# Exponentials with their sums on ScalarE, the sign of converted weights as an integer, and another order in the first block

## The chip, the core and the metric

The kernel runs on one core of a Trainium2 chip. The core has five engines that take their instructions in order, each from its own queue: PE (TensorE, matmuls and transposes), DVE (VectorE), ACT (ScalarE), POOL (GpSimd) and SP, which here only issues DMAs. PE writes to PSUM; DVE and ACT read and write PSUM and SBUF; POOL has SBUF alone. Engines wait for each other by semaphores. The metric is the device time of one execution in microseconds; lower is better.

## What is computed

Attention without a score matrix, and then two feed-forward layers, in float32, for 8 batches of 576 tokens, 8 heads of 64 columns:

```python
q_s = exp(q - max(q, axis=-1)); q_s = q_s / (sum(q_s, axis=-1) + 1e-9)     # over the 64 columns
k_s = exp(k - max(k, axis=2));  k_s = k_s / (sum(k_s, axis=2) + 1e-9)      # over the 576 tokens
kv  = einsum('bhsd,bhse->bhde', k_s, v)
x   = einsum('bhsd,bhde->bhse', q_s, kv)            # then (4608, 512): heads side by side
x   = (silu(x @ w_gate) * (x @ w_val)) @ w_out      # d_ff 1536
out = elu(x @ w_in) @ w_out2                        # d_ff 2048
```

The weights come as float64. Inputs q, k and v are float32.

## The kernel before

The tokens are cut into 9 blocks of 512. Every product is made of three matmuls: each factor is held as a high part, rounded to TensorE's float32 form, and the remainder, and high x high, high x remainder and remainder x high are summed in PSUM (`mm3` and `proj`, L632 to L636 for the projections, L613 to L615 for the second product). The feed-forward layers come in three passes over the 9 blocks: "a" is the first half of d_ff of the first layer, "b" its second half, "2" the second layer. Pass "a" is where attention lies: while block i goes through its six steps ff of three parts s (gate projection, val projection, the second product of the step before), the attention of block i + 1 is put between them by the tables `PLAN0` (for i = 0), `PLAN1` and `PLAN`, which name the part (ff, s) at which a step is issued. So the instructions of an engine stand in the order in which this program writes them; nothing moves later.

The weights are converted on the chip, 68 chunks of 128x512, by `conv()`, which in block 0 is called at each part and takes one chunk a stage further. The stages: `conv_scale` (ACT) multiplies the upper 32-bit word of each float64, read as a float32, by 2^-112, which shifts its exponent; `conv_bits` (DVE, L154, L157, L161) shifts the result left by three bits, puts the sign bit back and fills in the top bits of the lower word; `conv_split` makes the high part on ACT (L182) and the remainder on POOL (L183).

The attention steps of a block: `kmax` is the maximum of keys over tokens of a partition (DVE), `k1` transposes it on PE and reduces it (DVE), `k2` spreads it by PE over the partitions again (mb); `ks` subtracts it from the keys (ke), `kexp` is the exponential (ACT), and `kv` 40 small matmuls for two halves of the heads, whose result is divided by the sum into bd. For the queries: `qmax` (DVE), `qsub` (POOL in the first two blocks), `qexp` (ACT), `qsum` (DVE), `qnorm` (POOL there), then transposes `qT` and the product `xT`, whose result is split into x and its remainder.

Block 0's attention is `first_block()`, written out by hand ahead of the stream: nothing but small work can be on PE until x is there. The key's and value's halves (heads 0 to 3 and 4 to 7) are loaded one after the other on SP's queue. The first gate projection (`lo_last`) takes x's high parts first.

Of the kernel before, what the change touches and what calls it, by code (L numbers as in the profile page):

```python
# [7 lines left out]
FP32 = mybir.dt.float32  # L8
F32R = mybir.dt.float32r
U32 = mybir.dt.uint32  # L10
I64 = mybir.dt.int64
ACTF = mybir.ActivationFunctionType
ALU = mybir.AluOpType
AX = mybir.AxisListType
# [3 lines left out]
def kernel(  # L18
# [23 lines left out]
    nc = tc.nc  # L42
    B, H, S, D = q.shape
# [7 lines left out]
    NREST = S - 512  # L51
    NW1, NW2, NRAW, NCG, NCD = 20, 12, 3, 3, 4
# [79 lines left out]

    def conv_scale(wait=0):
        n = stage["scale"]
        if n >= stage["load"] or n >= stage["bits"] + NCG or calls[0] < loaded[n] + wait:
            return
        stage["scale"] += 1
        g = cv_p.tile([128, 512], U32, tag="cg", name="cg", bufs=NCG)
        nc.scalar.activation(
            out=g.bitcast(FP32), in_=raws[n][:, :, 1].bitcast(FP32), func=ACTF.Copy,  # L140
            scale=2.0 ** -112,
        )
        gs[n] = g

    def conv_bits():
        n = stage["bits"]
        if n >= stage["scale"] or n >= free[0] + NCD:
            return  # L150
        stage["bits"] += 1
        g = gs.pop(n)
        s = ps_c.tile([128, 512], U32, tag="c", name="c")
        nc.vector.tensor_scalar(  # L154
            s, g, 3, 0x7FFFFFFF, op0=ALU.logical_shift_left, op1=ALU.bitwise_and
        )
        nc.vector.scalar_tensor_tensor(  # L157
            out=s, in0=g, scalar=0x80000000, in1=s, op0=ALU.bitwise_and, op1=ALU.bitwise_or
        )
        d = cv_p.tile([128, 512], U32, tag="cd", name="cd", bufs=NCD)  # L160
        nc.vector.scalar_tensor_tensor(  # L161
            out=d, in0=raws.pop(n)[:, :, 0], scalar=29, in1=s,
            op0=ALU.logical_shift_right, op1=ALU.bitwise_or,
        )
        ds[n] = d

    def conv_split(eng):
        n = stage["split"]
# [98 lines left out]
    def kmax(b):  # L267
        t, r = k_t[b]
        m = at1.tile([128, H, D], FP32, tag="km", name="km")
        nc.vector.tensor_tensor(m, t[:, :, 0, :], t[:, :, 1, :], op=ALU.max)  # L270
        nc.vector.tensor_tensor(m, m, t[:, :, 2, :], op=ALU.max)
        nc.vector.tensor_tensor(m, m, t[:, :, 3, :], op=ALU.max)
        nc.vector.tensor_tensor(m[0:NREST], m[0:NREST], r, op=ALU.max)
        km_t[b] = m

# [69 lines left out]
            op=ALU.mult,  # L345
        )

    qr_t, qn_t = {}, {}
# [12 lines left out]

    def qexp(t, n):
        x = q_t[t][:, 4 * n:4 * n + 4]
        nc.scalar.activation(out=x, in_=x, func=ACTF.Exp)

    def qsum(t, n):
        h = slice(4 * n, 4 * n + 4)
        nc.vector.tensor_reduce(out=qr_t[t][:, h], in_=q_t[t][:, h], axis=AX.X, op=ALU.add)

    def qnorm(t, n, eng=None):  # L370
        h = slice(4 * n, 4 * n + 4)
        x = q_t[t][:, h]
        r = qr_t[t][:, h]
# [97 lines left out]
    def first_block():  # L471
# [22 lines left out]
        def km(n, eng):  # L494
            h = hs[n]
            eng.tensor_tensor(m[:, h], kt[:, h, 0, :], kt[:, h, 1, :], op=ALU.max)
            eng.tensor_tensor(m[:, h], m[:, h], kt[:, h, 2, :], op=ALU.max)
            eng.tensor_tensor(m[:, h], m[:, h], kt[:, h, 3, :], op=ALU.max)
            eng.tensor_tensor(m[0:NREST, h], m[0:NREST, h], kr[:, h], op=ALU.max)

        def turn(n, src):
            ps = bank()[:, 0:256]
# [28 lines left out]
        def vcopy(n):  # L531
            h = slice(4 * n, 4 * n + 4)
            src = st.rearrange("p h j d -> p j h d")
            nc.scalar.activation(out=vtile[:, 0:4, h, 0:D], in_=src[:, :, h], func=ACTF.Copy)

        load(kt, k, 0)
        nc.sync.dma_start(out=kr, in_=k[0, :, 512:S, :].rearrange("h p d -> p h d"))
        load(kt, k, 1)
        load(st, v, 0)
        load_half(0)  # L540
        load_half(1)
# [10 lines left out]
        nc.gpsimd.memset(ke[NREST:128, 4], 0.0)  # L552
        nc.gpsimd.memset(vtile[NREST:128, 4], 0.0)
        nc.gpsimd.memset(vtile[:, :, :, D:D + 1], 1.0)
        km(0, nc.vector)
        p0 = turn1(0)
        km(1, nc.vector)
        p1 = turn1(1)
        p0 = kmc(0, p0)
        p1 = kmc(1, p1)  # L560
        vcopy(0)
        ksub(0, p0)
        qmax(0, 0)
        qsub(0, 0, nc.gpsimd)
        kexp(0)
        kv(0, 0, 0)
        qmax(0, 1)
        qsub(0, 1, nc.gpsimd)
        vcopy(1)
        qexp(0, 0)  # L570
        ksub(1, p1)
        kexp(1)
        kv(0, 1, 0)
        qsum(0, 0)
        qexp(0, 1)
        qnorm(0, 0, nc.gpsimd)
        conv_scale()
        conv_scale()
        kv(0, 0, 1)
        qT(0, 0)  # L580
        qT(0, 2)
        qsum(0, 1)
        qnorm(0, 1, nc.gpsimd)
        kv(0, 1, 1)
        conv_bits()
        conv_split(nc.gpsimd)
        qT(0, 1)
        qT(0, 3)
        xT(0, 0, 0)
        conv_scale()  # L590
        xT(0, 0, 1)
        xT(0, 1, 1)
        load_q(1)
        xT(0, 2, 0)
        conv_bits()
        conv_split(nc.gpsimd)
        xT(0, 2, 1)
        xT(0, 3, 1)
        conv_scale()
# [174 lines left out]
    def load_next(ph, i):  # L774
# [14 lines left out]
        "kmax": (4, 2), "qmax": (5, 2),  # L789
    }  # L790
    PLAN0 = {
# [16 lines left out]
    def steps(i):  # L808
        t, u = i + 1, i + 2
        e = nc.gpsimd if i == 0 else nc.vector  # L810
        st = {}
        if i == 1:
            st["store0"] = lambda: store_x(0)
        if t < B:
            st["kmax0"] = lambda: kmax(t)
            st["k1"] = lambda: k1(t)
            st["k2"] = lambda: (k2(t), t + 1 < B and t > 1 and load_k(t + 1))
            st["ks0"] = lambda: ks(t, (0, 1), nc.gpsimd)
            st["ks1"] = lambda: (ks(t, (2, 3), nc.gpsimd), ks(t, (4,), nc.vector))
            st["load_v"] = lambda: load_v(t)  # L820
            st["load_k2"] = lambda: load_k(t + 1)
            st["load_q2"] = lambda: load_q(t + 1)
            st["load_v2"] = lambda: load_v(t + 1)
            st["kexp"] = lambda: kexp(t)
            st["kv0"] = lambda: kv(t, 0)
            st["kv1"] = lambda: (
                kv(t, 1),
                t + 1 < B and t > 1 and load_v(t + 1),
            )
        if t < NB:  # L830
            st["qmax0"] = lambda: (qmax(t, 0), qmax(t, 1))
            st["sub0"] = lambda: qsub(t, 0, e)
            st["sub1"] = lambda: qsub(t, 1, e)
            st["exp0"] = lambda: qexp(t, 0)
            st["exp1"] = lambda: qexp(t, 1)
            st["sum"] = lambda: (qsum(t, 0), qsum(t, 1))
            st["norm0"] = lambda: qnorm(t, 0, e)
            st["norm1"] = lambda: (qnorm(t, 1, e), t + 1 < NB and t > 1 and load_q(t + 1))
            for n in range(KD):
                st[f"qT{n}"] = lambda n=n: qT(t, n)  # L840
                st[f"xT{n}"] = lambda n=n: xT(t, n)
            st["store"] = lambda: store_x(t)
        if u < B:
# [137 lines left out]
```

## Time and profile before

| | us |
|---|---|
| median of 3 runs (1791.27 to 1791.88) | 1791.45 |
| profiled execution, its own time | 1792.23 |
| its span, first to last instruction | 1790.5 |
| PE busy | 1752.0 |
| DVE busy | 924.9 |
| ACT busy | 856.0 |
| POOL busy | 173.1 |

PE is the engine that is busy nearly all the time. The span begins with some 30 us in which it has only small matmuls; the first matmul of the stream starts at 29.63. An engine's busy share says nothing on what it delays; for that the waits of PE, and the chain that leads to each, have to be read.

### The profile page before, as it was taken

The page shows a single profiled execution, that of the slowest core. Times are in us where ns is not written, and L with a number is a line of the kernel's source. Part 1 is how long each engine was busy: PE and PEld are TensorE (multiplying, and loading weights), DVE is VectorE, ACT ScalarE, POOL GpSimd, SP SyncE. Part 2 cuts the span into 40 slices and gives each one's busy share as a digit, 9 for nine tenths or more (in the row PEclk, how much of TensorE's full clock was granted, in tenths as well). Part 3 has the DMA queues.
Part 4 walks back from the last instruction along what each step waited for, and adds up shares of the span by engine and source line. Part 5 has one row for each costly group of instructions (what it writes and reads, how often), then busy time and mean ns, then how long its engine had stood idle before and what let it go on. Part 6 is the DMA issues. An engine that isn't in the chain of part 4 may idle for free.

```text
span 1790.5 us, 21046 instructions
## 1 busy us (share of the span) xinstructions
PE 1752.0 (98%) x8448; PEld 1433.3 (80%) x8448; DVE 924.9 (52%) x1383; ACT 856.0 (48%) x1466; POOL 173.1 (10%) x135
## 2 busy tenths in 40 slices
PE   6799999999999999999999999999999999999999
PEld 4577888888888888888888788888888888888887
DVE  6866567556577666534346744333433343334343
ACT  4563544534465454433334654444444444444444
POOL 3630000000022222111113300000000000000000
PEclk9899999999999999999999999999999999999999
DMA  9274534341255344433334401010101010101000
GB/s 273 80 228 102 147 100 124 105 114 65 78 192 176 129 171 168 165 118 118 118 118 164 174 3 71 1 71 1 71 1 71 1 71 1 71 1 71 1 24 24
DMA packets 103106, 169.13 MB, mean 94 GB/s; under 512 B 41696, under 2 KB 80608, under 8 KB 98528
## 3 DMA queue, kind: packets, MB, share of 16 engines
q1 hardware_dynamic: 103008, 167.79, 28.5%
q8 instruction: 66, 1.08, 0.3%
q14 instruction: 32, 0.26, 0.0%
HBM read 111.15 MB, written 56.62 MB: 94 GB/s over the span
## 4 chain that ended last, share of the span: by engine, by line
PE 90%; issue 2%; DVE 2%; POOL 2%; ACT 2%; DMA 1%; SPq 1%; POOLq 0%; DVEq 0%; ACTq 0%
PE a L632 17%; PE a L633 17%; PE a L636 17%; PE y L613 12%; PE y L615 12%; PE y L614 12%; POOL w L183 1%; PE t L451 1%; DMA ev<-in_v 1%; PE t L390 1%; SPq L242 0%; PE t L331 0%; PE c L331 0%; DMA xs<-x 0%; POOL ke L310 0%
## 5 line engine op out<-in xcount | busy, mean ns | idle before, releaser
L632 PE MATMUL a<-x,w 128*128 128x512 f32 x1432 | 562.8, 393 | 1.5 <-DVE th L688 1.2
L633 PE MATMUL a<-x,w 128*128 128x512 f32 x1432 | 558.9, 390 | 0.7 <-POOL x L463 0.7
L636 PE MATMUL a<-x,w 128*128 128x512 f32 x1432 | 382.8, 389 | 0.0
L645 ACT ACTIVATE g<-th 128x512 fp32r<-128x512 f32 x252 | 159.3, 632 | 442.4 <-DVE th L673 226.3
L632 PEld LDWEIGHTS a<-x,w 128*128 128x128 f32 x1432 | 269.8, 188 | 60.7 <-DVE th L688 2.0
L633 PEld LDWEIGHTS a<-x,w 128*128 128x128 f32 x1432 | 269.8, 188 | 56.2 <-POOL x L463 1.2
L636 PEld LDWEIGHTS a<-x,w 128*128 128x128 f32 x1432 | 268.8, 188 | 55.8
L685 DVE SCALAR_TENSOR_TENSOR th<-e,th 128x512 f32<-128x512 f32 x144 | 100.9, 701 | 356.6 <-ACT e L684 356.6
L651 DVE TENSOR_TENSOR g<-th,g 128x512 fp32r<-128x512 f32 x246 | 176.2, 716 | 136.7 <-ACT g L645 136.6
L613 PE MATMUL y<-w,g 128*128 128x512 f32 x576 | 224.1, 389 | 0.0
L615 PE MATMUL y<-w,g 128*128 128x512 f32 x576 | 224.1, 389 | 0.0
L614 PE MATMUL y<-w,g 128*128 128x512 f32 x576 | 224.1, 389 | 0.0
L667 DVE SCALAR_TENSOR_TENSOR th<-th,e 128x512 f32<-128x512 f32 x108 | 77.3, 715 | 274.6 <-ACT th L663 274.6
L682 ACT ACTIVATE e<-a 128x512 f32<-128x512 f32 x144 | 86.1, 598 | 183.4 <-PE a L636 183.4
L613 PE MATMUL y<-g,w 128*128 128x512 f32 x432 | 171.8, 398 | 0.0
L660 ACT ACTIVATE e<-a 128x512 f32<-128x512 f32 x107 | 64.1, 599 | 224.4 <-PE a L636 224.3
L614 PE MATMUL y<-g,w 128*128 128x512 f32 x432 | 169.0, 391 | 0.0
L615 PE MATMUL y<-g,w 128*128 128x512 f32 x432 | 169.0, 391 | 0.0
L183 POOL TENSOR_TENSOR w<-cd,w 128x512 fp32r<-128x512 f32 x68 | 91.6, 1349 | 624.8 <-ACT w L182 604.1
L613 PEld LDWEIGHTS y<-w,g 128*128 128x128 f32 x576 | 108.2, 188 | 22.6
L615 PEld LDWEIGHTS y<-w,g 128*128 128x128 f32 x576 | 108.1, 188 | 22.5
L614 PEld LDWEIGHTS y<-w,g 128*128 128x128 f32 x576 | 108.1, 188 | 22.3
(137 smaller groups left out, 1705.7 us busy)
## 6 DMA issues: line engine op xcount, KB each, us to landing
xs<-x SPq DMA_DIRECT2D x9, 2048.0 KB, 6.3
x<-xs SPq DMA_DIRECT2D x36, 512.0 KB, 6.2
ys<-yst SPq DMA_DIRECT2D x36, 512.0 KB, 3.7
x<-ys SPq DMA_DIRECT2D x36, 512.0 KB, 7.2
raw<-in_moe_w_out SPq DMA_DIRECT2D x26, 512.0 KB, 3.3
yp<-ev SPq DMA_DIRECT2D x9, 1024.0 KB, 4.0
ev<-yp SPq DMA_DIRECT2D x9, 1024.0 KB, 7.9
raw<-in_moe_w_in SPq DMA_DIRECT2D x16, 512.0 KB, 4.0
```

The source lines that it names most:

```text
L183: eng.tensor_tensor(w[:, 1, :], df, w[:, 0, :].bitcast(FP32), op=ALU.subtract)
L613: nc.tensor.matmul(out=ps, lhsT=wh, rhs=xh, start=first, stop=False)
L614: nc.tensor.matmul(out=ps, lhsT=wh, rhs=xl, start=False, stop=False)
L615: nc.tensor.matmul(out=ps, lhsT=wl, rhs=xh, start=False, stop=last)
L632: nc.tensor.matmul(out=ps, lhsT=wh, rhs=x[:, c, 0, :], start=(c == 0), stop=False)
L633: nc.tensor.matmul(out=ps, lhsT=wh, rhs=x[:, c, 1, :], start=False, stop=False)
L636: nc.tensor.matmul(out=ps, lhsT=wl, rhs=x[:, c, 0, :], start=False, stop=(c == KD - 1))
L645: nc.scalar.activation(out=gt[:, 0, :], in_=src, func=ACTF.Copy)
L651: (eng or nc.vector).tensor_tensor(gt[:, 1, :], src, gt[:, 0, :].bitcast(FP32), op=ALU.subtract)
L667: nc.vector.scalar_tensor_tensor(out=t, in0=t, scalar=1.0, in1=e, op0=ALU.add, op1=ALU.mult)
L682: nc.scalar.activation(out=e, in_=h, func=ACTF.Relu, scale=-1.0)
L685: nc.vector.scalar_tensor_tensor(out=t, in0=e, scalar=1.0, in1=t, op0=ALU.add, op1=ALU.mult)
```

## The change

Four things change. In the conversion, ACT makes, beside the scaled word, a second tile by a Prelu with a large slope, written as an int32: positive and negative values saturate there, so that with the shifted word it gives the sign; DVE then needs two operations for a chunk where it had three. In blocks 0 and 1 the queries' subtraction, exponential and sum become 32 ACT operations a block: `qexp_sum` takes one head and one of four token groups, 64 columns, with the negated maximum as a bias and the sum as a second output (`accum_out`). The keys' maximum of batch 1 is one reduction. And `first_block` and `PLAN0` are in another order; the copies of v move from ACT to POOL, and products of `qnorm` in the first block from POOL to DVE.

```diff
     def conv_scale(wait=0):
...
+        d = cv_p.tile([128, 512], U32, tag="cd", name="cd", bufs=NCD)
+        nc.scalar.activation(
+            out=d.bitcast(I32), in_=g.bitcast(FP32), func=ACTF.Prelu, scale=2.0 ** 90,
+            alpha=2.0 ** 100,
+        )
...
     def conv_bits():
...
-        nc.vector.tensor_scalar(
-            s, g, 3, 0x7FFFFFFF, op0=ALU.logical_shift_left, op1=ALU.bitwise_and
-        )
         nc.vector.scalar_tensor_tensor(
-            out=s, in0=g, scalar=0x80000000, in1=s, op0=ALU.bitwise_and, op1=ALU.bitwise_or
-        )
+            out=s, in0=g, scalar=3, in1=d, op0=ALU.logical_shift_left, op1=ALU.bitwise_or
+        )
...
     def kmax(b):
...
+        if b == 1:
+            nc.vector.tensor_reduce(
+                out=m, in_=t.rearrange("p h j d -> p h d j"), axis=AX.X, op=ALU.max
+            )
...
+    def qmaxn(t, n):
+        qmax(t, n)
+        h = slice(4 * n, 4 * n + 4)
+        nc.vector.tensor_scalar(qr_t[t][:, h], qr_t[t][:, h], -1.0, None, op0=ALU.mult)
+
+    def qexp_sum(t, hs):
+        x, r = q_t[t], qr_t[t]
+        if t not in qs_t:
+            qs_t[t] = at1.tile([128, H, 4], FP32, tag="qs", name="qs")
+        for h in hs:
+            for j in range(4):
+                nc.scalar.activation(
+                    out=x[:, h, j], in_=x[:, h, j], func=ACTF.Exp, bias=r[:, h, j:j + 1],
+                    accum_out=qs_t[t][:, h, j:j + 1],
+                )
...
     def vcopy(n):
...
-            nc.scalar.activation(out=vtile[:, 0:4, h, 0:D], in_=src[:, :, h], func=ACTF.Copy)
+            nc.gpsimd.tensor_copy(vtile[:, 0:4, h, 0:D], src[:, :, h])
 
         load(kt, k, 0)
+        load(kt, k, 1)
         nc.sync.dma_start(out=kr, in_=k[0, :, 512:S, :].rearrange("h p d -> p h d"))
-        load(kt, k, 1)
...
-        km(0, nc.vector)
+        km(0)
+        km(1)
+        nc.vector.tensor_tensor(m[0:NREST], m[0:NREST], kr, op=ALU.max)
...
     PLAN0 = {
...
-        "exp0": (1, 2), "ks1": (2, 0), "sub1": (2, 0), "exp1": (2, 1), "kexp": (2, 1),
+        "k2": (2, 0), "ks0": (2, 0), "ea2": (2, 0), "ks1": (2, 1), "ea3": (2, 1),
...
-            st["ks1"] = lambda: (ks(t, (2, 3), nc.gpsimd), ks(t, (4,), nc.vector))
+            st["ks1"] = lambda: ks(t, (2, 3, 4), nc.gpsimd)
...
+            st["qmaxn"] = lambda: (qmaxn(t, 0), qmaxn(t, 1))
+            for n in range(4):
+                st[f"ea{n}"] = lambda n=n: qexp_sum(t, (2 * n, 2 * n + 1))
```

On ACT, in the first block, before (ke are the keys' exponentials, q the queries', cg the scaled word, vtile the values, qT the transposed queries, x the first projection's input):

```order
L534 ACTIVATE vtile<-ev 128x4x4x64
L529 ACTIVATE ke<-ke 128x256 x4
L529 ACTIVATE ke<-ke 64x256
L534 ACTIVATE vtile<-ev 128x4x4x64
L364 ACTIVATE q<-q 128x1024
L529 ACTIVATE ke<-ke 128x256 x4
L529 ACTIVATE ke<-ke 64x256
L364 ACTIVATE q<-q 128x1024
L139 ACTIVATE cg<-raw 128x512 x2
```

On ACT, at the same place in the first block, now (qs are the sums, cd the Prelu's output):

```order
L555 ACTIVATE ke<-ke 128x256 x4
L555 ACTIVATE ke<-ke 64x256
L388 ACTIVATE q,qs<-q,qr 128x64 x16
L140 ACTIVATE cg<-raw 128x512
L147 ACTIVATE cd<-cg 128x512
L555 ACTIVATE ke<-ke 128x256 x4
L555 ACTIVATE ke<-ke 64x256
L388 ACTIVATE q,qs<-q,qr 128x64 x16
L425 ACTIVATE qT_313<-t 128x512
```

The copies of v are gone from ACT, each exponential of the queries is 16 instructions, and the first chunk's two conversion operations stand ahead of the second half of the keys.

On the same engine, ahead of the second batch's keys in block 0's stream (w is a weight's high part, e and th belong to the gates, g is the split gate product, mb the spread maximum), before:

```order
L299 ACTIVATE mb<-t 128x512
L364 ACTIVATE q<-q 128x1024
L182 ACTIVATE w<-cd 128x512
L139 ACTIVATE cg<-raw 128x512
L660 ACTIVATE e<-a 128x512
L661 ACTIVATE th<-a 128x512
L662 ACTIVATE e<-e 128x512
L663 ACTIVATE th<-th 128x512
L182 ACTIVATE w<-cd 128x512
L139 ACTIVATE cg<-raw 128x512
L364 ACTIVATE q<-q 128x1024
L315 ACTIVATE ke<-ke 128x2048
```

On ACT, at the same place of the stream, now:

```order
L309 ACTIVATE mb<-t 128x512
L388 ACTIVATE q,qs<-q,qr 128x64 x8
L187 ACTIVATE w<-cd 128x512
L140 ACTIVATE cg<-raw 128x512
L147 ACTIVATE cd<-cg 128x512
L388 ACTIVATE q,qs<-q,qr 128x64 x8
L668 ACTIVATE g<-th 128x512
L187 ACTIVATE w<-cd 128x512
L140 ACTIVATE cg<-raw 128x512
L147 ACTIVATE cd<-cg 128x512
L325 ACTIVATE ke<-ke 128x2048
L326 ACTIVATE ke<-ke 64x512
```

Two other groups of eight stand ahead of mb; kexp (L325) comes behind all 32, and behind the split of the third g, which had stood after it.

## Rows read from the trace of the kernel before

**Rows 1.** The page: busy time, share of the span and instructions of each engine.
```profile
PE 1752.0 (98%) x8448; PEld 1433.3 (80%) x8448; DVE 924.9 (52%) x1383; ACT 856.0 (48%) x1466; POOL 173.1 (10%) x135
```
**Rows 2.** Waits of PE: what waited for what: us in total, times, longest.
```profile
PE t L280 <- DVE km L273: 7.6, 1, 7.6
PE t L331 <- ACT ke L315: 3.1, 1, 3.1
...
PE a L632 <- DVE th L688: 1.2, 2, 0.6
...
PE t L390 <- DVE bd L343: 0.9, 1, 0.9
```
**Rows 3.** Stretches: us, busy us of each engine (instructions), granted clock, DMA.
```profile
0.00:34.52 34.52, 18.61 (x133) 12.45 (x133) 20.94 (x46) 16.69 (x30) 11.55 (x15) 1.00 1.02 284
34.52:75.29 40.77, 27.41 (x106) 21.48 (x104) 37.60 (x51) 20.73 (x35) 23.59 (x17) 0.83 0.48 121
75.29:86.77 11.48, 10.58 (x108) 8.52 (x109) 8.98 (x18) 6.25 (x12) 9.20 (x6) 0.85 0.27 91
```
**Rows 4.** Timeline of PE: start, us, line, out<-in, count, idle before.
```profile
25.36 1.97 PE L390 MATMUL y<-ident,qn 128*128 128x128 f32 x8 [0.52 <-POOL qn L378]
...
31.12 3.56 PE L625 MATMUL y<-x,w 128*128 128x512 f32 x10 [0.54 <-ACT x L433]
34.52 0.40 PE L632 MATMUL y<-x,w 128*128 128x512 f32 x1
...
75.29 1.88 PE L331 MATMUL t<-vtile,ke 128*64 128x65 f32 x40 [3.15 <-ACT ke L315]
```
**Rows 5.** Timeline of DVE, block 0 and the next.
```profile
43.28 0.69 DVE L154 TENSOR_SCALAR c<-cg 128x512 uint32<-128x512 uint32 x1
44.00 0.69 DVE L157 SCALAR_TENSOR_TENSOR c<-cg,c 128x512 uint32<-128x512 uint32 x1
...
46.48 1.64 DVE L271 TENSOR_TENSOR km<-km,k 128x512 f32<-128x512 f32 x1
...
107.70 0.69 DVE L271 TENSOR_TENSOR km<-km,k 128x512 f32<-128x512 f32 x1
```
**Rows 6.** Timeline of DVE, first block.
```profile
13.70 2.33 DVE L354 TENSOR_REDUCE qr<-q 128x16 f32<-128x1024 f32 x2
```
**Rows 7.** Timeline of ACT, first block and the first gate.
```profile
18.94 1.63 ACT L529 ACTIVATE ke<-ke 128x256 f32<-128x256 f32 x5
20.47 1.04 ACT L364 ACTIVATE q<-q 128x1024 f32<-128x1024 f32 x1
...
28.95 1.08 ACT L433 ACTIVATE x<-y 128x512 fp32r<-128x512 f32 x2 [0.99 <-PE y L451]
...
38.26 0.63 ACT L662 ACTIVATE e<-e 128x512 f32<-128x512 f32 x1
38.78 0.63 ACT L663 ACTIVATE th<-th 128x512 f32<-128x512 f32 x1
```
**Rows 8.** Groups by shape, ACT, up to 75.3: busy us, mean ns.
```profile
L946 ACT ACTIVATE warm<-warm 128x1 f32<-128x1 f32 x1 | 0.2, 203 | 0.0
...
L315 ACT ACTIVATE ke<-ke 128x2048 f32<-128x2048 f32 x1 | 1.9, 1894 | 0.0
```
**Rows 9.** Timeline of ACT in pass "2": a Tanh that needs the Relu.
```profile
1201.36 0.60 ACT L682 ACTIVATE e<-a 128x512 f32<-128x512 f32 x1 [1.40 <-PE a L636]
1201.99 0.63 ACT L683 ACTIVATE th<-e 128x512 f32<-128x512 f32 x1
```
**Rows 10.** Timeline of POOL, block 0.
```profile
45.85 1.72 POOL L651 TENSOR_TENSOR g<-th,g 128x512 fp32r<-128x512 f32 x1
...
70.44 1.90 POOL L360 TENSOR_TENSOR q<-q,qr 128x1024 f32<-128x1024 f32 x1
```
**Rows 11.** The tile raw up to 40 us: duration and start of issues; time to landing.
```profile
L125 SPq DMA_DIRECT2D raw<-in_moe_w_gate x3: 1100/1256/1276, 9.1 to 36.3; - x3
...
DMA to landing us min/median/max: 8.5/10.1/11.7
```

More of the change, by code (lines that the diff above doesn't have):

```diff
@@ L11 @@
 I64 = mybir.dt.int64
+I32 = mybir.dt.int32
 ACTF = mybir.ActivationFunctionType
@@ L134, in conv_scale @@
         n = stage["scale"]
-        if n >= stage["load"] or n >= stage["bits"] + NCG or calls[0] < loaded[n] + wait:
+        if n >= stage["load"] or n >= stage["bits"] + NCG or n >= stage["split"] + NCD or calls[0] < loaded[n] + wait:
             return
@@ L142, in conv_scale @@
         )
+        d = cv_p.tile([128, 512], U32, tag="cd", name="cd", bufs=NCD)
[3 more added lines that the diff above has]
+        )
         gs[n] = g
+        ds[n] = d
     def conv_bits():
         n = stage["bits"]
-        if n >= stage["scale"] or n >= free[0] + NCD:
+        if n >= stage["scale"]:
             return
@@ L153, in conv_bits @@
         s = ps_c.tile([128, 512], U32, tag="c", name="c")
-        nc.vector.tensor_scalar(
-            s, g, 3, 0x7FFFFFFF, op0=ALU.logical_shift_left, op1=ALU.bitwise_and
-        )
-        nc.vector.scalar_tensor_tensor(
-            out=s, in0=g, scalar=0x80000000, in1=s, op0=ALU.bitwise_and, op1=ALU.bitwise_or
-        )
-        d = cv_p.tile([128, 512], U32, tag="cd", name="cd", bufs=NCD)
+        d = ds[n]
+        nc.vector.scalar_tensor_tensor(
+            out=s, in0=g, scalar=3, in1=d, op0=ALU.logical_shift_left, op1=ALU.bitwise_or
+        )
         nc.vector.scalar_tensor_tensor(
@@ L164, in conv_bits @@
         )
-        ds[n] = d
     def conv_split(eng):
@@ L269, in kmax @@
         m = at1.tile([128, H, D], FP32, tag="km", name="km")
-        nc.vector.tensor_tensor(m, t[:, :, 0, :], t[:, :, 1, :], op=ALU.max)
-        nc.vector.tensor_tensor(m, m, t[:, :, 2, :], op=ALU.max)
-        nc.vector.tensor_tensor(m, m, t[:, :, 3, :], op=ALU.max)
+        if b == 1:
+            nc.vector.tensor_reduce(
+                out=m, in_=t.rearrange("p h j d -> p h d j"), axis=AX.X, op=ALU.max
+            )
+        else:
+            nc.vector.tensor_tensor(m, t[:, :, 0, :], t[:, :, 1, :], op=ALU.max)
+            nc.vector.tensor_tensor(m, m, t[:, :, 2, :], op=ALU.max)
+            nc.vector.tensor_tensor(m, m, t[:, :, 3, :], op=ALU.max)
         nc.vector.tensor_tensor(m[0:NREST], m[0:NREST], r, op=ALU.max)
@@ L346, in kv @@
         )
-    qr_t, qn_t = {}, {}
+    qr_t, qn_t, qs_t = {}, {}, {}
     def qmax(t, n):
@@ L372, in qnorm @@
         x = q_t[t][:, h]
-        r = qr_t[t][:, h]
+        r = (qs_t if t in qs_t else qr_t)[t][:, h]
         nc.vector.tensor_scalar(r, r, 1e-9, None, op0=ALU.add)
@@ L492, in load, with km @@
             )
-        def km(n, eng):
+        def km(n):
             h = hs[n]
[L496 to L499, printed above, removed]
+            nc.vector.tensor_tensor(m[:, h], kt[:, h, 0, :], kt[:, h, 1, :], op=ALU.max)
+            nc.vector.tensor_tensor(m[:, h], m[:, h], kt[:, h, 2, :], op=ALU.max)
+            nc.vector.tensor_tensor(m[:, h], m[:, h], kt[:, h, 3, :], op=ALU.max)
         def turn(n, src):
@@ L554, in first_block @@
         nc.gpsimd.memset(vtile[:, :, :, D:D + 1], 1.0)
-        km(0, nc.vector)
+        km(0)
+        km(1)
+        nc.vector.tensor_tensor(m[0:NREST], m[0:NREST], kr, op=ALU.max)
         p0 = turn1(0)
-        km(1, nc.vector)
         p1 = turn1(1)
@@ L562, in first_block @@
         ksub(0, p0)
-        qmax(0, 0)
-        qsub(0, 0, nc.gpsimd)
+        qmaxn(0, 0)
         kexp(0)
         kv(0, 0, 0)
-        qmax(0, 1)
-        qsub(0, 1, nc.gpsimd)
+        ksub(1, p1)
+        qmaxn(0, 1)
+        qexp_sum(0, range(0, 4))
         vcopy(1)
-        qexp(0, 0)
-        ksub(1, p1)
+        conv_scale()
         kexp(1)
         kv(0, 1, 0)
[L574 to L578, printed above, removed]
+        qnorm(0, 0)
         kv(0, 0, 1)
+        qexp_sum(0, range(4, 8))
         qT(0, 0)
         qT(0, 2)
-        qsum(0, 1)
-        qnorm(0, 1, nc.gpsimd)
+        conv_bits()
         kv(0, 1, 1)
+        qnorm(0, 1)
+        conv_scale()
         conv_bits()
-        conv_split(nc.gpsimd)
         qT(0, 1)
         qT(0, 3)
+        conv_split(nc.gpsimd)
         xT(0, 0, 0)
-        conv_scale()
         xT(0, 0, 1)
         xT(0, 1, 1)
+        conv_split(nc.gpsimd)
+        conv_scale()
         load_q(1)
         xT(0, 2, 0)
-        conv_bits()
-        conv_split(nc.gpsimd)
         xT(0, 2, 1)
```

4 rows, old and new, of the table PLAN0 are left out of this document.

## The prediction, as it was put on record

> **What bounds the kernel now.** I read the page first: TensorE is busy for 98% of the span [rows 1], so only a stretch in which it waits can give or take time. The list of its waits came next. They are few: the two largest inside the stream are 7.6 us for the maxima of the second batch's keys (km, L273) and 3.1 us for their exponentials (ke, L315), both in the first block of tokens; of what comes after 121 us, only two waits for th (L688) of 0.6 us each stand there [rows 2]. The table by stage says the same: of 121 us TensorE works 18.6 of the first 34.5 and 27.4 of the next 40.8 [rows 3]; behind that it is full. So the change is decided in the first 90 us, in two pieces: the start, up to the val projection at 34.52, and from there to kv0, the 40 small matmuls at 75.29 that wait for ke [rows 4].
>
> **What costs nothing.** Each of the 68 weight chunks loses one of three VectorE operations (0.72 from start to start) [rows 5] and gains a Prelu of 512 columns on ScalarE. Over the program this moves some 49 us off VectorE and 35 us on to ScalarE. After 121 us neither shows: TensorE has hardly a wait there [rows 2], and ScalarE is busy 48% [rows 1]. The new maximum of the keys reads 2048 elements in one reduction, twice the 1.2 us that 1024 take, where the second of three operations alone took 1.64 [rows 5, 6]. It also stands two steps earlier than the transposes that need it, so the wait of 7.6 us goes. What is late next is the question.
>
> **The price on which all hangs.** In the first two blocks POOL subtracts, ScalarE exponentiates (two of 1.04 us a block [rows 7]) and VectorE sums. All this becomes 32 exponentials a block on ScalarE, each of 64 columns, with the maximum as a bias read from memory and a sum written out. The trace has no such instruction. From the rows: 1.04 us for 1024 columns and 1.89 for 2048 give 0.83 ns a column, so 64 columns take 0.24 us; the Exp and the Abs of a gate start 0.52 apart at 0.63 each, so 0.11 overlap and the least step is 0.134 us [rows 7, 8]. The sum must be read out after the last element, by a small operation (128x1 took 203 ns [rows 8], so about 0.10 in step). Where one ScalarE operation needs the other's result, the overlap is lost: Tanh starts 0.63 after a Relu of 0.60 [rows 9]. So: 0.24, a gap of 0.03 and 0.10 make 0.37 us each. The ends are 0.134 (bias and read-out free) and 0.46 (nothing overlaps: 0.241 + 0.203 + gaps). I take 0.37, since Relu to Tanh is the nearest row. In 16 that is 5.9 us, where one exponential of 1.04 stood.
>
> The Trainium skill, ScalarE: Activation LUTs, section "What ACT_TABLE_LOAD costs", says that a per-partition pointer operand adds about 93 ns to an ACTIVATE. No row here has such an operand. By that rule my 0.37 would be 0.46 and the time by the sum below 1801 us; with the read-out overlapped it would be 0.33, and 1794.
>
> **The start.** The exponentials of the first half can start when the first maximum, which started at 13.70 (1.2), and a negation of 16 columns (an estimate: 0.2, as 128x1 on ScalarE) are through, at 15.1 [rows 6, 8]. The reordered key loads leave that start where it is: both halves' maxima are one chain now, but the second half lands about as much sooner as the remainder lands later. The two copies of v go to POOL, which has nothing else to do there; the later one is not needed before the second kv. From 15.1 ScalarE holds in a row: 16 exponentials (5.9), scale and Prelu of a chunk (0.65 + 0.52 = 1.17: the Prelu needs the scale's result, so as Relu to Tanh), the keys' exponentials (1.63 [rows 7]), and 16 more (5.9): it ends at 29.7. Before, the second exponential ended at 21.5 [rows 7]. Then two small operations and the product on VectorE (1.2; L360 in place) take 1.85 until the transposes start, against 3.85 before (25.36 [rows 4]) over a sum and POOL. From there to the first x copy it was 3.6 (28.95), and 2.17 more until TensorE resumed at 31.12 [rows 4, 7]; into these the new order puts one weight split (0.55) and a Prelu with its wait (0.6). So 29.7 + 1.85 + 3.6 + 3.3 = 38.5. The rest of the gate projection took 3.4, since its last matmuls waited for the x remainders behind a conversion on VectorE; that conversion now stands ahead, so ten matmuls of 0.23 do: val at 40.8. **Start: 6.3 us later.** TensorE and all its followers are queued behind it; on SP the load of the second block's q, which waits for the product's end (31.6), goes some 5 us later with the rest of its queue, and its maxima come 20 us after that.
>
> **From val to kv0.** ScalarE ends the x copies at 39.0 and must pass, in order, all that stands ahead of kexp: 10 scales with Prelu (11.7), 9 weight splits at 0.53 (4.8), three sets of four for the gates at 0.52 (6.3), three splits of g (1.7), mb (0.5), 32 exponentials (11.8) and kexp itself (1.9): 38.7. It idles some 2.9: 1.1 for the first chunk's bits, 0.5 for the first g and 1.3 for the second, whose val stands on VectorE behind four conversions, the maxima of keys (3.0 with its remainder) and of queries (2.7). kexp ends at 80.6, not 75.3, and kv0 starts there. TensorE reaches it with time to spare: eight groups of twelve matmuls at 0.23 are 22, with waits inside some 30, so at 71. POOL's subtractions stand between mb at about 68 and kexp's start, and ScalarE has ten us of other work there. **kv0: 5.4 later**: the start's loss of 6.3 less 0.9. From kv0 to the next gate it was 11.48 [rows 3], 0.9 of it a wait for bd [rows 2] which VectorE, with less to do, has ready: 4.5 in all remains. What follows goes at TensorE's pace as before.
>
> The sum against the profiled execution's own time: 1792.23 + 4.5 = 1796.7 (its span of 1790.5 and 1.7 around it). It lies 0.8 above the median shown, so I say 1796.0 for a median. Since 24 exponentials in this piece and 32 in the start are on ScalarE's chain (the first eight fall into its idle time), every 0.01 us of their price moves the time by 0.56.
>
> **Rivals.** (1) *The read-out overlaps*, 0.23 to 0.35 us each. For it: most neighbours on ScalarE overlap by 0.1 [rows 7]. Against: Relu to Tanh. At 0.30 the time is 1796.0 - 3.9 = 1792: no change that can be told (0.2%, or 3.6 us, is what a measurement here can tell).
> (2) *Faster*: the price is near the least step, below 0.23. Then the start gains from POOL and VectorE leaving the chain, and kexp no longer waits for POOL's L360, which ended only at 72.34 [rows 10]. At 0.134 the sum gives -8.7, but the scale of the first chunk, ahead of the keys' exponentials, then comes to its turn at 17.2, and its data took 8.5 to 11.7 after an issue at 9.1 [rows 11]: some 1.7 come back. 1784.5.
> (3) *VectorE is held by POOL.* The new first step of the conversion reads two tiles from SBUF, the old ones one (the other from PSUM). L271, also two from SBUF, took 1.64 beside POOL and 0.69 at 107.7, where POOL was idle at its start [rows 5, 10]. The three such steps ahead of the second val would each lose up to 0.95 there: val, the split of g and kexp 2.9 later, 1798.9. Against: POOL is busy only 23.6 of these 40.8 us [rows 3]. The Trainium skill, SBUF — State Buffer, section "Who interferes with whom", says that a VectorE instruction with two SBUF inputs contends with a GpSimd instruction that reads SBUF. The pair of rows agrees; by the rule the time is the 1798.9 of this rival.
>
> **Numbers.** Forecast 0.35; overlap 0.31; faster 0.22; held by POOL 0.12. The ends of the price give 1784.5 and 1801; with POOL's hold on top of the upper one it is 1804. I take 1784 to 1804. Slower by over 0.2%: forecast and rival 3, 0.47; within: 0.31; faster: 0.22.
>
> **What would show it.** In the changed profile: the start to start of the small exponentials (0.37; under 0.3 or over 0.45 moves the time as said); the end of the first 32 at 29.7; val at 40.8; the largest waits of TensorE inside the stream for ke, not km, and kv0 at 80.6; the new first conversion step at 0.69, or above 1 beside POOL. ScalarE should be near full from 15 to 80 us. If it has gaps of several us there, my chain is not the one that binds, and the forecast is wrong even if the time is right.

## The result, and the profile after

The changed kernel took 1816.64 us (median of 4 runs, 1816.22 to 1816.77) beside 1791.38 for the kernel before (4 runs, 1791.27 to 1791.88): 1.0139 times as long, 95% interval 1.0127 to 1.0152. The direction was the forecast's, the size was not: 25.3 us slower, where 4.5 were expected and 1804 was the top of the range.

To see where the 25 us arise, the start of each of the 252 gates on ACT (the Relu of each projection) is compared with the same gate before. In the profiled executions the changed kernel is later by 3.7 at the first gate, 5.31 at kv0, 6.07 at the fifth gate (96.17 against 90.10), then 5.95 with no change up to 510 us. In the times of the kernel before, from 519 to 584 us (the last block of pass "a" and the first of "b") it loses 3.45 more, from 959 to 1038 us (the last block of pass "b", the first steps of pass "2") 14.6 more, and nothing outside. In both stretches weights are converted while TensorE is full. So 18.05 of 24.0 us lie where the prediction said that nothing would show. In what follows the three are called the front, the middle and the late stretch.

The page of the changed kernel, the line that answers to [rows 1]: VectorE gave away 20 us, ScalarE took on 56.

```profile
PE 1756.6 (97%) x8448; PEld 1433.5 (79%) x8448; DVE 905.0 (50%) x1313; ACT 911.8 (50%) x1656; POOL 167.1 (9%) x132
```

PE's waits in the changed kernel, as [rows 2] (us in total, times, longest). The wait for km (L273, 7.6) is gone. The waits for th, before only two of 0.6, are now the largest inside the stream, together with a longer wait for ke (7.1 for 3.1). Of the 13.1 at L693, 7.3 lie in the front (the 6.4 behind the maxima of keys), 1.0 around 550 us and 4.8 behind 960 us; the 5.0 at L711 lie behind 960 us too:

```profile
PE a L655 <- DVE th L693: 13.1, 7, 6.4
...
PE t L341 <- ACT ke L325: 7.1, 1, 7.1
...
PE a L655 <- DVE th L711: 5.0, 3, 3.8
```

PE's timeline of the changed kernel, beside [rows 4] (start, duration, idle before): transposes of the second half 29.23 (25.36 before), val projection 39.24 (34.52), kv0 80.60 (75.29).

```profile
29.23 1.94 PE L417 MATMUL y<-ident,qn 128*128 128x128 f32 x8 [3.96 <-DVE qn L405]
...
39.24 0.39 PE L655 MATMUL y<-x,w 128*128 128x512 f32 x1
...
80.60 2.44 PE L341 MATMUL t<-vtile,ke 128*64 128x65 f32 x40 [7.14 <-ACT ke L325]
```

ACT's timeline of the changed kernel: the small exponentials, and the keys' exponential that kv0 waits for. Each exponential has a second instruction that reads the sum out; the next exponential starts before that ends, so one costs 0.333 from start to start (14.23 to 14.56).

```profile
13.88 0.35 ACT L388 ACTIVATE q<-q,qr 128x64 f32<-128x64 f32 x1 [0.93 <-DVE qr L380]
...
14.23 0.33 ACT L388 ACTIVATE q<-q,qr 128x64 f32<-128x64 f32 x1
14.47 0.19 ACT L388 ACTIVATION_READ_ACCUMULATOR q<-q,qr 128x1 f32 x1
14.56 0.33 ACT L388 ACTIVATE q<-q,qr 128x64 f32<-128x64 f32 x1
...
78.66 1.89 ACT L325 ACTIVATE ke<-ke 128x2048 f32<-128x2048 f32 x1
```

The late stretch, by windows of 940 to 1080 us (busy us of PE, PEld, DVE, ACT, POOL with instructions; clock; DMA). First the kernel before, then the changed one: PE falls from full to 127.9 of 140, while DVE and ACT are busy about half of the time in both.

```profile
940.00:1080.00 140.00, 138.46 (x608) 113.43 (x607) 85.55 (x123) 75.51 (x132) 35.50 (x26) 1.00 0.31 109
```

```profile
940.00:1080.00 140.00, 127.91 (x543) 102.67 (x543) 72.90 (x100) 78.06 (x138) 35.02 (x26) 0.98 0.32 110
```

What holds PE there stands on ACT. One step of the changed kernel, from one split of g to the next:

```profile
985.15 0.63 ACT L668 ACTIVATE g<-th 128x512 fp32r<-128x512 f32 x1 [1.24 <-DVE th L696]
985.69 0.61 ACT L187 ACTIVATE w<-cd 128x512 fp32r<-128x512 f32 x1
986.21 0.66 ACT L140 ACTIVATE cg<-raw 128x512 f32<-128x512 f32 x1
987.80 0.63 ACT L147 ACTIVATE cd<-cg 128x512 int32<-128x512 f32 x1 [0.93 <-POOL w L188]
...
990.36 0.63 ACT L147 ACTIVATE cd<-cg 128x512 int32<-128x512 f32 x1 [0.85 <-POOL w L188]
990.90 0.58 ACT L683 ACTIVATE e<-a 128x512 f32<-128x512 f32 x1
...
995.28 0.63 ACT L668 ACTIVATE g<-th 128x512 fp32r<-128x512 f32 x1 [2.27 <-DVE th L696]
```

The Prelu waits for POOL twice in a step, and for each of the 14 chunks of the late stretch (14.0 us in all). Its output cd comes from a ring of four buffers. Before, VectorE took the buffer in a later stage (`conv_bits`), and only one whose split had been issued in an earlier call of `conv()` (the count `free[0]`). Now ScalarE takes it, and the buffer is that of the chunk four back, whose split `conv()` has issued just ahead. So ScalarE starts the split, then stands until POOL has made the remainder from that same buffer, here from 986.38 to 987.77:

```profile
986.38 1.39 POOL L188 TENSOR_TENSOR w<-cd,w 128x512 fp32r<-128x512 f32 x1 [0.33 <-ACT w L187]
```

Behind the Prelu stand the next gate's four operations, and PE waits for what follows from them. Its steps come 10.1 us apart, where the 36 matmuls of one take 8.16 in the kernel before (gates at 959.40 and 967.56):

```profile
984.38 0.50 PE L655 MATMUL a<-x,w 128*128 128x512 f32 x1 [1.58 <-DVE th L693]
994.50 0.50 PE L655 MATMUL a<-x,w 128*128 128x512 f32 x1 [1.65 <-DVE th L693]
```

The middle stretch loses with no wait for POOL. The same two splits of g on ACT in the kernel before, at 540 us:

```profile
539.48 0.63 ACT L645 ACTIVATE g<-th 128x512 fp32r<-128x512 f32 x1 [2.27 <-DVE th L673]
...
541.59 0.63 ACT L182 ACTIVATE w<-cd 128x512 fp32r<-128x512 f32 x1 [0.40 <-DVE cd L161]
...
543.24 0.60 ACT L660 ACTIVATE e<-a 128x512 f32<-128x512 f32 x1 [0.46 <-PE a L636]
...
547.64 0.63 ACT L645 ACTIVATE g<-th 128x512 fp32r<-128x512 f32 x1 [2.27 <-DVE th L673]
```

A step of ScalarE is a loop: four gate operations, 2.27 of waiting for the three of VectorE that need them, the split of g, two chunks. Of its 8.16 us only the waits of 0.40 and 0.46 are free, 0.86 in all; the 2.27 is no free time, since what it waits for hangs on ScalarE itself. Two Prelus of some 0.55 and more do not fit. In the changed kernel the same step takes 8.53, and only the 2.27 is left of its waits:

```profile
548.76 0.63 ACT L668 ACTIVATE g<-th 128x512 fp32r<-128x512 f32 x1 [2.27 <-DVE th L696]
...
549.82 0.65 ACT L140 ACTIVATE cg<-raw 128x512 f32<-128x512 f32 x1
550.57 0.63 ACT L147 ACTIVATE cd<-cg 128x512 int32<-128x512 f32 x1
...
557.29 0.63 ACT L668 ACTIVATE g<-th 128x512 fp32r<-128x512 f32 x1 [2.27 <-DVE th L696]
```

### The profile page after: what moved, and what is told of

It is laid out like the page before. It is cut to its first block, busy times and chain, and to the rows that moved or that the text cites. A ratio compares the mean times of both kernels' runs of the same rounds, so it can differ in the third digit from the quotient of the medians.

```text
span 1814.5 us, 21214 instructions
## 1 busy us (share of the span) xinstructions
PE 1756.6 (97%) x8448; PEld 1433.5 (79%) x8448; DVE 905.0 (50%) x1313; ACT 911.8 (50%) x1656; POOL 167.1 (9%) x132
## 5 line engine op out<-in xcount | busy, mean ns | idle before, releaser
L655 PE MATMUL a<-x,w 128*128 128x512 f32 x1432 | 565.6, 395 | 20.2 <-DVE th L693 13.1
L674 DVE TENSOR_TENSOR g<-th,g 128x512 fp32r<-128x512 f32 x246 | 180.9, 735 | 136.8 <-ACT g L668 136.7
```

What stands on the lines that cost most here:

```text
L655: nc.tensor.matmul(out=ps, lhsT=wh, rhs=x[:, c, 0, :], start=(c == 0), stop=False)
L674: (eng or nc.vector).tensor_tensor(gt[:, 1, :], src, gt[:, 0, :].bitcast(FP32), op=ALU.subtract)
```

## The experiments

The losses below are those of the profiled execution against that of before, by gates; front, middle, late. Medians stand with the interval of their ratio to before. A profiled execution can differ from the median by some us: the conversion with its Prelu in PSUM, alone, is 12.6 by its gates and 15.9 by its median.

| kernel | median, us | ratio | front | middle | late |
|---|---|---|---|---|---|
| changed | 1816.6 | 1.0127 to 1.0152 | 5.95 | 3.45 | 14.6 |
| conversion alone | 1809.3 | 1.0085 to 1.0115 | 0.33 | 3.1 | 13.9 |
| attention alone | 1795.1 | 1.0012 to 1.0030 | 3.6 | 0 | -0.6 |
| changed, ring of 5 | 1803.9 | 1.0051 to 1.0084 | 5.8 | 3.4 | 3.4 |
| the same, conversion ahead | 1801.85 | 1.0044 to 1.0074 | 5.7 | 1.7 | 2.2 |
| changed, Prelu in PSUM | 1814.6 | 1.0113 to 1.0147 | 13.7 | 5.8 | 2.9 |
| that conversion alone | 1807.3 | 1.0071 to 1.0101 | 5.0 | 5.8 | 1.9 |
| block 1 alone | 1792.7 | 0.9999 to 1.0018 | 0.05 | 0 | -0.1 |
| half of the start | 1793.8 | 1.0005 to 1.0024 | 1.85 | 0 | -0.2 |
| before + scratch Prelu | 1801.4 | 1.0040 to 1.0070 | 1.4 | 2.8 | 4.7 |
| attention + scratch Prelu | 1807.5 | 1.0077 to 1.0104 | 8.0 | 2.7 | 5.2 |
| part of the new order, big exponentials | 1792.1 | 0.9998 to 1.0016 | 1.4 | 0 | 0.4 |
| order mended | 1786.9 | 0.9967 to 0.9985 | -4.95 | 0 | -0.7 |
| order mended, small exponentials | 1792.1 | 0.9996 to 1.0013 | 0.5 | 0 | -0.7 |

**The two halves, and the ring.** Three kernels: the changed one with five buffers for cd (and two for cg, to make room; the order of instructions is the same on all engines), the kernel before with the new conversion alone, and the changed kernel with the old conversion.

```diff
-    NW1, NW2, NRAW, NCG, NCD = 20, 12, 3, 3, 4
+    NW1, NW2, NRAW, NCG, NCD = 20, 12, 3, 2, 4
...
-        d = cv_p.tile([128, 512], U32, tag="cd", name="cd", bufs=NCD)
+        d = cv_p.tile([128, 512], U32, tag="cd", name="cd", bufs=NCD + 1)
```

> The changed kernel with five buffers for the Prelu's output (cd) and two for the scaled word (cg) in place of four and three; every engine's instructions stand in the same order. Theory A (ScalarE's Prelu takes the buffer whose remainder POOL is just making, and stands 0.84 us for it, twice a step at the end of the first layer, so that a step takes 10.06 us where TensorE needs 8.16): the wait goes, the step becomes 8.5 us as around 540 us, five steps win 1.5 each and the first steps of the second layer some 3 more: 1805 to 1808 us. Theory B (the Prelu's own 0.65 us for each chunk is what makes the step too long, the wait is hidden in ScalarE's idle time): less than 3 us won, 1813 or more. Theory C (all is lost in the first 100 us): no change, 1816.

> The kernel before with the new conversion alone (Prelu on ScalarE, two VectorE operations); attention and first block as before. Theory A: the loss behind 500 us (18 of the 25 us) is the conversion's and comes in full, while the first block wins 0 to 4 us, since VectorE is full there (37.6 of 40.8 us) and sheds 0.72 a chunk: 1805 to 1810. Theory C (the loss is that of the small exponentials and the new order): within 3 us of the kernel before, 1788 to 1794.

> The changed kernel with the old conversion (no Prelu, three VectorE operations). Theory A: nothing is lost behind 500 us; in the first 100 us ScalarE sheds ten Prelus of 0.65 from its chain ahead of the second keys' exponentials but VectorE takes up ten operations of 0.72, so the 6 us lost there shrink to 1 to 5: 1792 to 1796. Theory C: 1810 or more.

The times of the conversion alone and the attention alone fell where theory A has them, though the front of the first lost 0.33 where 0 to 4 were to be won. The fifth buffer gave a little more than expected. It takes 12.7 of the 25.3 us away by the medians, 11.45 by the gates, nearly all late. On ACT the Prelu of the same stretch no longer waits:

```profile
983.63 0.63 ACT L147 ACTIVATE cd<-cg 128x512 int32<-128x512 f32 x1
984.17 0.62 ACT L187 ACTIVATE w<-cd 128x512 fp32r<-128x512 f32 x1
```

The conversion is 17.3 of the loss by itself, the attention 3.0; together they lose 3.7 more than the sum, most of it in the front and late.

**The loop of ScalarE.** With five buffers the middle still lost 3.4. If that is the loop, conversion work put into the wait of 2.27 must win it back.

```diff
+                    if s == 1 and i == NB - 1:
+                        conv()
                     if s == 1:
                         silu_val(t, val, (ph, i, f))
```

(The call stood behind `silu_val` and `split_lo` before.)

> The five buffers of e1, and in the last block of the first layer the conversion call of the val part issued ahead of the split of g, into the 2.3 us in which ScalarE waits for VectorE. Theory A says that after the wait for POOL is gone the step is 8.5 us, because ScalarE's conversions (1.8 us a chunk) stand in one chain with the gate: with one of the two in the idle time the step falls to TensorE's 8.16 and the late loss is all but gone: 1797 to 1801, that is the 6 us of the start. If the chain is another one, no better than e1.

It won 2.1 and missed its range by 0.9: 1.7 in the middle and 1.1 late by the gates. A step in the middle was 0.15 over 8.16 instead of some 0.36. The direction is the loop's, the size was over-rated. Of what is left late, 2.5 us with five buffers and 2.3 with the conversion ahead arise within two gates, around 990 us. There ScalarE waits 2.7 and 5.1 us for the landing of a weight chunk. That this wait makes them is read from the traces and was not tested.

The direct test: the kernel before with a Prelu per chunk into a tile that nobody reads, so in the main ScalarE's time alone, and the same with the new attention. To make room, both have two buffers for cg instead of three.

```diff
+        z = cv_p.tile([128, 512], U32, tag="cz", name="cz", bufs=1)
+        nc.scalar.activation(
+            out=z.bitcast(I32), in_=g.bitcast(FP32), func=ACTF.Prelu, scale=2.0 ** 90,
+            alpha=2.0 ** 100,
+        )
```

> The kernel before, and per chunk a Prelu more on ScalarE, into a scratch tile that nobody reads (two buffers for cg to make room); the conversion is that of before. So there is ScalarE's time alone, with no wait on the ring and no new operation of VectorE. Theory A (what the ring and the hold don't explain is ScalarE's own time): front 0 to 1, middle 3 to 4 (0.36 a step for the steps with two chunks, as in the changed kernel), late 1.5 to 3: 1796 to 1799. Rival (ScalarE's time costs nothing where it is half idle; ring and VectorE make all of the loss): 1791 to 1792.5.

> The new attention with the conversion of before, and the same Prelu into a scratch tile. The attention alone loses 3.6 in the front, the conversion alone 0.3, both together 5.9. Theory A (the 2.0 beyond the sum are ScalarE's time, since with the small exponentials it is nearly full there): front 5.2 to 6.2, in all 1799 to 1802. Rival (the 2.0 are VectorE held by POOL): front 3.6 to 4.4, in all 1797 to 1799.

Both lost more than theory A expected, and far more than the rival. ACT's step in the first of them, from g to g, is 8.40; its free 0.86 is used up and the two Prelus (1.10) stand 0.24 over:

```profile
535.50 0.63 ACT L651 ACTIVATE g<-th 128x512 fp32r<-128x512 f32 x1 [2.28 <-DVE th L679]
...
536.55 0.65 ACT L140 ACTIVATE cg<-raw 128x512 f32<-128x512 f32 x1
537.23 0.63 ACT L145 ACTIVATE cz<-cg 128x512 int32<-128x512 f32 x1
...
543.90 0.63 ACT L651 ACTIVATE g<-th 128x512 fp32r<-128x512 f32 x1 [2.27 <-DVE th L679]
```

In the changed kernel the same two Prelus stand 0.37 over: there each starts 0.75 after its scale (549.82 to 550.57), here 0.68 (536.55 to 537.23). So ScalarE's time makes most of the middle's loss, 2.8 of 3.45.

With the attention the front loses 8.0, where 3.6 and 1.4 would be 5.0. So a front loss beyond the sum arises without VectorE's new operation. These kernels keep three VectorE operations a chunk, which makes their fronts and late stretches no measure of the changed kernel's own. Their late loss also has a part from the two buffers of cg: at 964 us ScalarE waits 2.76 in the first of them for VectorE to read one, a wait that neither the kernel before nor the changed one has, and over which the kernel falls back by 0.95.

**The Prelu into PSUM.** Issued with the chunk's VectorE operations and written to their PSUM tile, the Prelu needs no buffer of cd, and the first VectorE operation has one SBUF input.

```diff
         s = ps_c.tile([128, 512], U32, tag="c", name="c")
+        nc.scalar.activation(
+            out=s.bitcast(I32), in_=g.bitcast(FP32), func=ACTF.Prelu, scale=2.0 ** 90,
+            alpha=2.0 ** 100,
+        )
         nc.vector.scalar_tensor_tensor(
-            out=s, in0=g, scalar=3, in1=d, op0=ALU.logical_shift_left, op1=ALU.bitwise_or
+            out=s, in0=g, scalar=3, in1=s, op0=ALU.logical_shift_left, op1=ALU.bitwise_or
```

> The whole change, but the Prelu is issued with the chunk's VectorE operations and writes into their PSUM tile; cd is written by VectorE alone, as before. So ScalarE never takes a buffer of the ring cd, and VectorE's first operation has one SBUF input. Theory A (in the late part ScalarE waits for POOL over the ring; in the first 100 us VectorE is held by POOL over two SBUF inputs): the late loss falls from 14.5 to the 2 to 3 that five buffers left, the front loss from 5.9 to 3 to 4.5, the middle stays at 3.5; 1800 to 1803. Theory B (the Prelu's own time on ScalarE is what costs, wherever it writes): as with five buffers, 1803.9 or more. Theory C (VectorE now waits for the Prelu in each chunk, behind ScalarE's other work, and passes that on): front above 7, over 1805.

> The kernel before with that conversion alone (Prelu into PSUM), attention as before. Theory A: front 0 to -1.5 (one VectorE operation a chunk less, no hold), middle +3, late +2: 1793 to 1796, against 1809.3 for the conversion with its output in the ring. Theory B: the Prelu's time itself costs the late 14: 1806 to 1810. Rival: with less on VectorE it is faster than before, below 1789.

By their medians both refute theory A; the second even falls into theory B's range. The gates say something else: the late loss went as theory A has it (13.9 to 1.9, 14.6 to 2.9), and a new one came in the front and the middle, theory C's. VectorE now waits for a Prelu that stands behind ScalarE's other work, and with one PSUM tile the next Prelu can wait for VectorE. First VectorE's waits for it in the first 130 us of this conversion alone (us in total, times, longest; from 500 to 595 us they are 19.3 in 16), then a row of ScalarE in the late stretch:

```profile
DVE c L161 <- ACT c L157: 26.3, 14, 5.2
```

```profile
986.41 0.60 ACT L157 ACTIVATE c<-cg 128x512 int32<-128x512 f32 x1 [0.49 <-DVE cd L165]
```

**The front: price or order.** One kernel has only block 1's part of the attention, one the new first block with only the first 16 small exponentials.

> The kernel before with the small exponentials, the one-reduction maximum and the new order in block 1 alone; the first block as before. Theory A (the attention's loss of 3.6 in the front is 2.7 of the start and 0.9 of block 1): 1791.5 to 1792.7, the wait for ke before kv0 of about 3 to 4.5. Rival (the 24 exponentials more on ScalarE in the stream cost by themselves, and in the run of both were hidden behind the later start): 1794 to 1797.

> The kernel before with the new first block in which only the first half of the queries' exponentials are the 16 small ones; the second half goes by POOL, one exponential and a sum on VectorE, as before; conversion and block 1 as before. Theory A (the price of the second 16, 5.3 us on ScalarE's chain against 1.04, makes the start's loss; the order gains): val 0.5 to 1.5 earlier than before, 1789.8 to 1791.3. Rival (the loss is of the order, not of the exponentials): val as late as with all of the new first block, 1794.

Block 1's part costs nothing that shows (its ratio holds 1, and its gates end 0.05 later). So, by difference, the start makes the loss of 3.6. The half start met its rival's time (val at 37.34; 34.52 before, 38.19 with the attention alone). But three conversion operations of VectorE, 2.1 us, stood ahead of the second half's norm in it, so it does not part the price from the order. Then the new order of loads, maxima, copies of v and products, with the big exponentials and with the conversion's operations where they stood before (part of its edit against the kernel before):

```diff
-        km(0, nc.vector)
+        km(0)
+        km(1)
+        nc.vector.tensor_tensor(m[0:NREST], m[0:NREST], kr, op=ALU.max)
         p0 = turn1(0)
-        km(1, nc.vector)
...
+        ksub(1, p1)
         qmax(0, 1)
+        vcopy(1)
         qsub(0, 1, nc.gpsimd)
-        vcopy(1)
         qexp(0, 0)
-        ksub(1, p1)
...
-        qnorm(0, 0, nc.gpsimd)
+        qnorm(0, 0)
```

> The kernel before with the new order of the first block's loads, maxima, v copies on POOL and products on VectorE, but both halves of the queries' exponentials as before (POOL subtracts, one exponential, VectorE sums); conversion and block 1 as before. Theory A (the start's loss is the price of the small exponentials on ScalarE's chain; the order itself gains): val 1.5 to 2.3 earlier, and the rest follows: 1789 to 1790. Second (the start gains, but block 1's keys and queries don't come sooner, so their chain takes it back by 100 us): val 1.5 to 2.3 earlier, 1791 to 1791.5. Rival (the order makes the loss): val later than before, 1793 or more.

Its val came 1.4 later, the rival's side, though its time lies between the ranges. ACT showed a reason: the first weight split still stood ahead of the last copies of qT, as in the kernel before. It waited 3.50 for its chunk, where it had waited 0.42 before, and held them.

```profile
27.17 0.63 ACT L182 ACTIVATE w<-cd 128x512 fp32r<-128x512 f32 x1 [3.50 <-DVE cd L161]
```

So the last pair mends that (split behind qT, second v copy on ScalarE, second chunk's bits ahead of x). Its two kernels differ by one edit, that of the small exponentials with the subtraction and the sums that they replace:

```diff
-        qmax(0, 0)
-        qsub(0, 0, nc.gpsimd)
+        qmaxn(0, 0)
...
-        qmax(0, 1)
-        qsub(0, 1, nc.gpsimd)
-        qexp(0, 0)
+        qmaxn(0, 1)
+        qexp_sum(0, range(0, 4))
...
-        qsum(0, 0)
-        qexp(0, 1)
+        qexp_sum(0, range(4, 8))
...
-        qsum(0, 1)
```

> As the order without small exponentials, mended in three places that its trace showed: the second copy of v on ScalarE (POOL's subtraction comes sooner and no longer lies beside VectorE's small operations), the first weight split behind the copies of qT (ScalarE stood 3.5 us before it), the second chunk's VectorE operations ahead of x. Theory A (with the big exponentials the start can be earlier than before; what the last run lost was the place of the split): transposes of the second half at 23 to 24 (25.36 before), val 1 to 2 earlier, 1789.5 to 1791. Rival (the new order of loads and maxima loses by itself): val at 35 or later, 1792 or more.

> That same order with one edit: the queries' subtraction, exponentials and sums of the first block are the 32 small exponentials. Theory A (their price on ScalarE's chain makes the start's loss: 32 x 0.333 = 10.7 us against 2 x 1.04, less what POOL and VectorE took): 3 to 5 later at val than the order mended without them, 1793.5 to 1796. Rival (the loss is of the order): the two within 1 us of each other.

PE's timeline, first with big exponentials (transposes of the second half, val, kv0), then with small ones:

```profile
23.58 1.94 PE L390 MATMUL y<-ident,qn 128*128 128x128 f32 x8 [0.88 <-DVE rs L340]
...
33.16 0.40 PE L636 MATMUL y<-x,w 128*128 128x512 f32 x1
...
70.35 1.44 PE L331 MATMUL t<-vtile,ke 128*64 128x65 f32 x40 [3.15 <-ACT ke L315]
```

```profile
28.97 1.94 PE L406 MATMUL y<-ident,qn 128*128 128x128 f32 x8 [3.68 <-DVE rs L340]
...
38.56 0.39 PE L648 MATMUL y<-x,w 128*128 128x512 f32 x1
...
75.76 1.44 PE L331 MATMUL t<-vtile,ke 128*64 128x65 f32 x40 [3.17 <-ACT ke L315]
```

All of it is 5.4 us later with the small ones, and the medians differ by 5.25: that is their price in the first block, in this order. Both theories A missed their ranges: the first kernel is 2.6 faster than expected, and in the second val comes 5.4 later, not 3 to 5, in a time below its range. The first kernel's val is 1.4 earlier than before and its kv0 4.9, since PE's wait for km (L273) before it fell from 7.6 to 4.1. The mended order is worth having: with the big exponentials it beats both kernels, 1786.88 us, 0.9976 of before (0.9967 to 0.9985). It is not the changed kernel's order. In that one no such pair was run, and why its front loses 3.6 with the small exponentials, where the mended order loses 0.5 with them, stays open.

## Why the prediction was right and wrong

**The step that failed is "What costs nothing. [...] After 121 us neither shows: TensorE has hardly a wait there [rows 2], and ScalarE is busy 48% [rows 1]."** It put the 68 Prelus at nothing; the new conversion costs 18 us behind 121 us. Two things were missed. The Prelu takes a ring buffer on another engine and at an earlier stage than before, so ScalarE gets a wait for POOL in each chunk of the late stretch (12.7 us by the kernel with five buffers). And 48% busy was read as room, where ScalarE's step is a loop through VectorE with 0.86 us free in 8.16 (the middle's 3.45 us, and some of the late loss that five buffers leave); that could be read from the trace of before. That TensorE had no waits there said only that nothing was late yet, not by how much.

**The price of one small exponential**: 0.37 forecast, 0.333 measured. The read-out overlaps the next exponential; rival 1's mechanism was there, at the upper part of its range. The read-out starts 0.24 after its exponential and the next exponential 0.09 after that (14.23, 14.47, 14.56). The Trainium skill, ScalarE: Activation LUTs, section "What ACT_TABLE_LOAD costs", puts about 93 ns on a pointer operand; with 0.24 for 64 columns that makes an estimate of 0.333 for the length of one exponential, and the trace agrees with 0.33.

**The start**: the exponentials began at 13.88 (forecast 15.1) and the last ended at 27.2 (29.7), but val came at 39.24 (40.8), 4.7 late instead of 6.3. Of the 2.5 won 0.9 was lost again behind it. After PE's wait of 3.96 its granted clock was at 0.50, its lower level (1.2 GHz), from 29 to 35 us, where it stayed at 1.00 before; with small exponentials in the mended order it stayed at 1.00 after a wait of 3.68. From the transposes to val it took 10.01, 9.16 and 9.59 us in these three. That the clock makes the difference is argued, not shown:

```profile
29.00:35.00 6.00, 5.77 (x25) 2.65 (x26) 2.65 (x5) 4.04 (x8) 1.39 (x2) 0.50 1.09 244
```

**From val to kv0**: kv0 at 80.60 was forecast to the tenth, but by luck, with errors that cancel: val came 1.6 sooner, and the stretch took 41.36, not 39.8. ScalarE's waits there made 4.9 us (0.98, 0.88, 1.02 and 2.06), where 2.9 were put. Its work came out as forecast, again by two errors: a scale with its Prelu took about 1.28 and not 1.17, ten times, which used up what 32 exponentials at 0.333 gave. The one reduction of the keys was put at 2.4 and took 3.87 (the first row of VectorE below), which alone is 1.5 on VectorE, ahead of the th for which PE then waited 6.4; the wait of 1.02 is for the chunk right behind it. That this makes up the 1.6 is argued, not shown: no run isolates the reduction.

**Behind kv0**: 0.9 was to come back. From kv0 to the split of g 0.66 did (11.58 before, 10.92 now), but from there to the next gate ScalarE passes two chunks with their Prelus, 4.65 instead of 3.23. 5.31 - 0.66 + 1.42 = 6.07: the same missed term again.

**Rival 3** (VectorE held by POOL) showed in the trace, larger than priced, but elsewhere. VectorE's timeline of the changed kernel, with the maximum of the keys and two first steps of the conversion:

```profile
47.07 3.87 DVE L276 TENSOR_REDUCE km<-k 128x512 f32<-128x2048 f32 x1
...
78.78 5.41 DVE L164 SCALAR_TENSOR_TENSOR c<-cg,cd 128x512 uint32<-128x512 uint32 x1 [2.82 <-ACT cd L147]
...
91.40 0.69 DVE L164 SCALAR_TENSOR_TENSOR c<-cg,cd 128x512 uint32<-128x512 uint32 x1
```

The steps ahead of the second val, where the rival had placed it, took 0.69 to 0.70. The 5.41 falls behind, and VectorE still delivered what the split of g needs 0.66 sooner, counted from kv0. Over the program 22 of the 68 first steps took over 0.8 us, 27 us in all beyond 0.69 each, which is most of why VectorE gave away 20 us and not the 49 of the prediction. Fourteen of them, 1.8 each from 591 to 713 us, cost nothing: the gates stay 9.40 later all along. What those in the front are worth stays open: of the kernels without the hold, those with the Prelu in PSUM brought a wait of their own, and the others have the old conversion. Rival 2 (faster) fell with the price.

**The range** reached to 1804 because it held every end of the small exponential's price and none for the Prelu's.

## What to carry to other kernels

An engine that is half idle may have no room: take its step in the full stream, count as free only those waits that do not hang on itself, and compare that with the work to be added; here 0.86 us of 8.16 were free, with ScalarE 48% busy over the program and 62% there (515 to 590 us). When an operation moves to another engine, look who allocates its output and at which stage: a ring that was deep enough for one engine becomes a wait on the other, and here one buffer more was worth 12.7 us. An exponential of 64 columns with its sum costs 0.333 us, so 32 of them (10.7 us) replace two big ones only where ScalarE has that time free on the chain.

## What was not expected of the hardware

- The read-out of a sum is an ACT instruction of its own, 0.19 us, of which the next exponential overlaps 0.10; 0.333 from start to start for 64 columns.
- A reduction over an axis with stride 64 (four token groups) took 3.87 us for 2048 elements, 1.9 ns each, where the one over contiguous columns took 1.21 for 1024.
- A VectorE operation with two SBUF inputs took 5.41 us instead of 0.69 while POOL ran four operations back to back from 78.05 to 83.6. With one of the inputs in PSUM (L161 of the two kernels with the Prelu there) it took 0.70 at most, in all 68 chunks. The Trainium skill, SBUF — State Buffer, section "Who interferes with whom", says that a VectorE operation with two SBUF inputs contends with a GpSimd one that reads SBUF, and one with at most one does not; both rows agree with it.
